# Five shared PSUM banks, one score task per chunk, and a new order of the work in a fused recurrence and feed-forward kernel

## The chip, the cores and the metric

The kernel runs on one core of a Trainium2 chip. The metric is device time in microseconds (us) of one execution; the median of three runs of the kernel before is 558.45 us (557.92 to 558.87). The core has a matrix engine (PE, with its weight loads shown apart as PEld), a vector engine (DVE), a scalar engine for activation functions (ACT), GpSimd (POOL) and a queue that issues transfers (SP). Matmuls write to PSUM, which has eight banks of 128 partitions by 512 fp32 values; DVE and ACT take results out of them.

## The reference

For each batch `b` (4) and head `h` (8) a linear recurrence runs over 768 steps with state 48 by 48, and its output tokens pass through a feed-forward net.

```python
mag = np.sqrt(a_re * a_re + a_im * a_im)
scale = np.minimum(mag, 0.999) / (mag + 1e-06)
a_re_n, a_im_n = (a_re * scale, a_im * scale)
for t in range(S):
    ar, ai = (a_re_n[:, :, t, :, None], a_im_n[:, :, t, :, None])
    new_re = ar * S_re - ai * S_im
    new_im = ar * S_im + ai * S_re
    S_re, S_im = (new_re + k_t v_t^T, new_im)
    y[:, :, t] = q_t @ S_re
...
h = x @ w_in                                       # 3072 x 384 by 384 x 2048
g = np.maximum(h, 0.0) + np.log1p(np.exp(-np.abs(h)))
return (g @ w_out).astype(np.float32)              # back to 3072 x 384
```

(The line with `k_t v_t^T` and the one with `q_t` stand for two einsums.)

## The kernel before, in words

**Tiling.** The 768 steps are cut into six groups of 128 steps. A group holds four chunks (one per batch) of 128 tokens, and after its four chunks the feed-forward net runs on the group's 512 tokens. The complex decay is turned into logarithms and angles by DVE and ACT (`pre`), which scale and rotate q and k; then a chunk is a small attention (`chunk`), and the group's 512 tokens go through `moe`.

**A chunk**, in the tiles' names: q and k are gathered by transfers into a room `qk`; k is transposed into `kt`. The scores of heads 0 to 3 and 4 to 7 (`score`, L655 in the first group, L659 later) are two tasks, each into one PSUM bank `att`. DVE multiplies a bank by a mask into `a` (`maskf`, L686). In all groups but the first, two small pieces of the bank go back into `qk`: the diagonal ones through DVE (`diag`, L674), the others by a copy that ACT or DVE does (`plain`, L696 or L679). Odd and even heads use other partitions, so each of the two is issued once for each parity. `ymm` (L722 and L726) forms the chunk's output, ACT or DVE copies its high part to `xt` (L745 or L744), DVE subtracts for the low part (L746). `kvmm` (L772 and L778) updates the state `s` (L787 or L790). Chunk matmuls after the first group have 32 output rows each (128*32 or 96*32 in the profile); the others use all of the array (128*128).

**The feed-forward net** is done in split precision. `mm1` has nine 128x512 matmuls (L817) for each of 16 slices `f` of the inner width, into a bank `h`. ACT takes abs, exp and log of it (L821 to L823), DVE reads the bank once more and completes the softplus (L832, or L826 in the first group), after which the bank is free; the result is split into `gh` and `gl` (L834 to L836). `mm2` has nine matmuls per slice (L852), accumulated over all 16 slices in three banks `o`. In the first group slices use an fp32 form (L849) instead. `filler` (L894) is a matmul whose result nobody uses.

**PSUM.** Eight banks: three `o`, two `h` and three `att` (`NATT = 3`).

**Order.** The functions only list tasks with their data dependences. `Planner.order` issues them in the sequence of a long list of numbers, `ORDER`: a number is a task, a suffix A or D moves it to ACT or DVE, `x` and `y` are fillers of 128 and 512 columns. Every engine then works strictly in that order, and waits by semaphores. When a task first uses a buffer it takes the slot that has been free longest, so the list also sets which bank a task gets. Durations given to `add` describe tasks to whoever makes the list, and change nothing in the program itself.

Of the kernel before, what the change touches and what calls it, by code (L numbers as in the profile page):

```python
# [40 lines left out]
NATT = 3  # L41
# [11 lines left out]
def slot(h):  # L53
    return h if h >= 6 else NI * (h % 2) + h // 2
# [115 lines left out]
class Prog:  # L170
# [39 lines left out]
    def masks(self):  # L210
# [15 lines left out]
        def copy():  # L226
# [6 lines left out]
            for room in FIXED["qk"]:  # L233
                G.memset(room[:QT, NI:], 0.0)
# [107 lines left out]
    def pre(self, si):  # L342
# [200 lines left out]
        return (arctan, a1(W), [t3]), (sincos, 2 * a1(W) + 0.05, [t4, t3]), turn, tail  # L543
# [4 lines left out]
    def chunk(self, si, c):  # L548
# [24 lines left out]
        if gc == 2:  # L573
            add("POOL", 3.0, lambda: nc.gpsimd.memset(qk()[:QT, NI:], 0.0), w=[(room, "z")])
# [10 lines left out]
        def heads(y):  # L585
            nc.sync.dma_start(qk()[QT * y : QT * y + 2 * D, 3 * y : 3 * y + 3].rearrange("p h n -> p (h n)"),
                              half()[D * y : D * y + D].rearrange("r (j n) -> r j n", j=2))

        def shared(y):
            nc.sync.dma_start(qk()[QT * y : QT * y + 2 * D, 6 + y],  # L590
                              half()[96 + 16 * y : 112 + 16 * y].rearrange("r (a n) -> r a n", a=2 * NI))
# [51 lines left out]
        am = []  # L643
        for j in range(2):
            psc = Buf(ps, "att", [P, 512], F32, f"sc{gc}_{j}", NATT)
            a = Buf(p, "g", [P, 4, P], F32, f"a{gc}_{j}", NG)
            am.append(a)

            def score(j=j, psc=psc):
                q = qk()  # L650
                for hh in range(4):
                    h = 4 * j + hh
                    r, k = slice(0, P if h % 2 else 2 * D), slot(h)
                    if first:
                        PE.matmul(psc()[:, hh * P : (hh + 1) * P], q[r, k, CH:], q[r, k, :CH], start=True, stop=True)  # L655
                        continue
                    for u in range(NQ):
                        f = QT * (u if h % 2 else NQ - 1 - u)
                        PE.matmul(psc()[QT * u : QT * (u + 1), hh * P + f : (hh + 1) * P],  # L659
                                  q[r, k, CH + f : CH + f + QT], q[r, k, f:CH], start=True, stop=True)  # L660

            def rows(t, z):
                return t[(P - QT, 0)[z] : (P, QT)[z]]

            def early(z, o, n, j=j):
                a, b = slot(4 * j + z), slot(4 * j + 2 + z)
                return rows(qk(), z)[:, a : b + 1 : b - a, o : o + n]

            def part(z, o, n, psc=psc):
                return rows(psc(), z).rearrange("p (x z t) -> p x z t", z=2, t=P)[:, :, z, o : o + n]  # L670
# [10 lines left out]
            def maskf(psc=psc, a=a):  # L681
                if first:
                    V.tensor_tensor(a(), psc().rearrange("p (x t) -> p x t", x=4),
                                    self.mask[:, 1][:, None].to_broadcast([P, 4, P]), ALU.mult)
                    return
                V.tensor_tensor(a()[:, :, : P - QT].rearrange("p (x z) t -> p x z t", z=2),  # L686
# [584 lines left out]
```

## Time and profile before

| | |
|---|---|
| median of three runs | 558.45 us |
| the profiled execution | 558.57 us, span 556.9 us |
| PE busy | 537.8 us (97%) |
| DVE busy | 451.8 us (81%) |
| ACT busy | 442.0 us (79%) |
| mean DMA rate | 155 GB/s |
| first feed-forward matmul | 52.76 us |
| last feed-forward matmul | 549.36 us |

Busy time of PE counts a matmul from its start to a modelled end, and neighbours overlap: how fast PE moves is read from the distance between starts. A wait in the profile is the idle time of an engine in front of an instruction, put down to what released it. A wait that a weight load (PEld) makes can be covered by matmuls that still run.

### The profile page before, as it was taken

The numbers are of one execution on the slowest core, as the hardware profiler recorded it, in microseconds if no ns is written. First come the engines' busy times: TensorE is split into PE (matmuls) and PEld (weight loads), VectorE is DVE, ScalarE is ACT, GpSimd is POOL, SyncE is SP. The second block draws the span as 40 slices with busy tenths as digits, with TensorE's granted clock in tenths as the row PEclk, the third lists the DMA queues.
The fourth block names the chain that finished last, engine by engine and source line by source line (L and its number), as shares of the span: only waits on it lengthen the run. The fifth ranks groups of instructions, "written<-read, shape, count | busy, mean of one in ns | idle before, by whom it ended". The sixth has DMA issues, their size and how long they took to land.

```text
span 556.9 us, 13372 instructions
## 1 busy us (share of the span) xinstructions
PE 537.8 (97%) x5432; PEld 419.1 (75%) x5432; DVE 451.8 (81%) x785; ACT 442.0 (79%) x776; POOL 10.5 (2%) x35
## 2 busy tenths in 40 slices
PE   4999999999999999999999999999999999999994
PEld 2689656756778887888887888788887888888883
DVE  5999999998989999998999989898898455433350
ACT  7995998788799998987987669858784665668792
POOL 7000000000000000000000000000000000000000
PEclk8899999999999999999999999999999999999998
DMA  8779905536346365176473473763626431045541
GB/s 313 278 195 312 400 26 125 204 119 189 111 159 173 131 172 189 54 189 200 105 229 89 116 189 84 192 195 112 150 75 177 128 86 58 28 126 145 157 140 61
DMA packets 49586, 86.04 MB, mean 155 GB/s; under 512 B 10224, under 2 KB 30448, under 8 KB 49520
## 3 DMA queue, kind: packets, MB, share of 16 engines
q1 hardware_dynamic: 49376, 84.89, 50.5%
q8 instruction: 43, 0.70, 0.5%
q10 hardware_dynamic: 144, 0.26, 0.1%
q14 instruction: 23, 0.19, 0.1%
HBM read 55.25 MB, written 7.86 MB: 113 GB/s over the span
## 4 chain that ended last, share of the span: by engine, by line
PE 46%; DVE 11%; ACT 3%; issue 1%; DMA 1%; SPq 0%; ACTq 0%; DVEq 0%
PE o L852 20%; PE h L817 20%; PE att L659 2%; DVE lt L832 2%; PE att L722 2%; DVE t L442 1%; DVE gl L836 1%; PE att L726 1%; DVE qk L679 1%; DVE kt L624 1%; PE att L778 1%; DVE qk L674 1%; DVE a L686 1%; ACT L945 1%; DMA qk<-x 1%
## 5 line engine op out<-in xcount | busy, mean ns | idle before, releaser
L817 PE MATMUL h<-xt,wi 128*128 128x512 f32 x864 | 216.6, 399 | 1.5 <-DVE lt L832 1.2
L817 PEld LDWEIGHTS h<-xt,wi 128*128 128x128 f32 x864 | 159.7, 188 | 42.9 <-DVE lt L832 4.5
L852 PE MATMUL o<-gh,wo 128*128 128x512 f32 x480 | 159.6, 396 | 0.0
L852 PEld LDWEIGHTS o<-gh,wo 128*128 128x128 f32 x480 | 90.1, 188 | 21.6 <-ACT o L876 0.2
L821 ACT ACTIVATE lt<-h 128x512 f32<-128x512 f32 x96 | 56.6, 592 | 62.5 <-PE h L817 54.3
L832 DVE SCALAR_TENSOR_TENSOR lt<-h,lt 128x512 f32<-128x512 f32 x80 | 54.5, 685 | 52.6 <-ACT lt L823 52.5
L852 PE MATMUL o<-gl,wo 128*128 128x512 f32 x240 | 94.4, 393 | 0.0
L823 ACT ACTIVATE lt<-lt,fixed 128x512 f32<-128x512 f32 x96 | 68.4, 718 | 1.7
L836 DVE TENSOR_TENSOR gl<-lt,gh 128x512 fp32r<-128x512 f32 x80 | 54.4, 684 | 8.9 <-ACT gh L835 4.1
L822 ACT ACTIVATE lt<-lt 128x512 f32<-128x512 f32 x96 | 59.9, 628 | 1.7
L852 PEld LDWEIGHTS o<-gl,wo 128*128 128x128 f32 x240 | 45.1, 188 | 10.2
L945 ACT ACT_TABLE_LOAD x34 | 43.6, 1283 | 0.6
L849 PE MATMUL o<-gf,raw_wo 128*128 128x512 f32 x96 | 43.2, 594 | 0.0
L442 DVE TENSOR_TENSOR_SCAN t<-hold,t 128x384 f32<-128x384 uint8 x40 | 36.1, 944 | 0.8
L659 PEld LDWEIGHTS att<-qk 128*32 128x32 f32 (+1 forms) x1280 | 25.2, 110 | 9.1 <-issue 3.7
L849 PEld LDWEIGHTS o<-gf,raw_wo 128*128 128x128 f32 x96 | 18.0, 190 | 18.5 <-issue 17.2
L659 PE MATMUL att<-qk 96*32 96x32 f32 (+7 forms) x1280 | 27.8, 234 | 1.2 <-DVE qk L679 0.5
L686 DVE TENSOR_TENSOR a<-att,mask 128x384 f32<-128x384 f32 x40 | 21.5, 543 | 3.4 <-PE att L659 1.7
L834 DVE TENSOR_SCALAR gh<-lt 128x512 fp32r<-128x512 f32 x49 | 20.3, 418 | 4.7 <-PE o L852 3.5
L540 DVE TENSOR_TENSOR x<-x,t 128x768 f32<-128x768 f32 x24 | 22.7, 950 | 0.3
L538 DVE TENSOR_TENSOR x<-x,t 128x768 f32<-128x768 f32 x24 | 22.5, 948 | 0.0
L722 PE MATMUL att<-qk,s 128*32 128x128 f32 x640 | 22.5, 274 | 0.0
(118 smaller groups left out, 720.9 us busy)
## 6 DMA issues: line engine op xcount, KB each, us to landing
x<-dense_dram SPq DMA_DIRECT2D x20, 768.0 KB, 6.6
qk<-x SPq DMA_DIRECT2D x48, 288.0 KB, 3.8
raw_wi<-w_in_dram SPq DMA_DIRECT2D x8, 768.0 KB, 10.1
raw_wo<-w_out_dram SPq DMA_DIRECT2D x8, 768.0 KB, 10.1
seen<-w_in_dram SPq DMA_DIRECT2D x16, 384.0 KB, 3.8
seen<-w_out_dram SPq DMA_DIRECT2D x16, 384.0 KB, 3.4
v<-vpad_dram SPq DMA_DIRECT2D x24, 224.0 KB, 3.9
qk<-x SPq DMA_DIRECT2D x48, 96.0 KB, 3.3
```

Of the source, the lines that this page charges most:

```text
L442: V.tensor_tensor_scan(out()[:, s], self.hold, inc()[:, s], 0.0, ALU.mult, ALU.add)
L659: PE.matmul(psc()[QT * u : QT * (u + 1), hh * P + f : (hh + 1) * P], q[r, k, CH + f : CH + f + QT], q[r, k, f:CH], start=True, stop=True)
L722: PE.matmul(o(G), s[:, w : w + 32], q[:, slot(h), :CH], start=prim and G < 4, stop=False)
L817: PE.matmul(h()[:, :n], w()[:, q, i, fs], xt()[:, x, i], start=k == 0, stop=k == 3 * NI - 1)
L821: add("ACT", a1(n) - 0.04, lambda: A.activation(tv(), h(), AF.Abs), r=[h], w=[t])
L822: add("ACT", a1(n), lambda: A.activation(tv(), tv(), AF.Exp, scale=-1.0), w=[t], tab="log")
L823: add("ACT", a1(n, 1), lambda: A.activation(tv(), tv(), AF.Ln, bias=self.one), w=[t], tab="log")
L832: add("DVE", d1(n), lambda: V.scalar_tensor_tensor(tv(), h(), 0.0, tv(), ALU.max, ALU.add), r=[h], w=[t])
L836: add("DVE", d1(n), lambda: V.tensor_tensor(gl(), tv(), gh().bitcast(F32), ALU.subtract), r=[t, gh], w=[gl])
L849: PE.matmul(acc[m]()[:, :n], v, gt[0](), start=f == 0, stop=f == NF - 1)
L852: PE.matmul(acc[m]()[:, :n], w()[:, wq, f % 2, ms], x(), start=f == 0 and q == 0, stop=f == NF - 1 and q == 2)
L945: nc.scalar.preload_act_table_set(TABLES[table])
```

## The change

1. `NATT` is 5: the `h` tiles of the feed-forward net and the attention tiles take banks from one pool of five. In the first group the running sums take a bank of it too.
2. A chunk's scores are one task into two banks, one for even and one for odd heads. `maskf`, `diag` and `plain` work on a parity each, so that `diag` and `plain` are one instruction of four heads where they were two of two heads. For that `slot` lays out `qk` by parity; `kslot` keeps the old layout for `kt`.
3. Durations told to the planner are changed in five places.
4. `ORDER` is another list.

```diff
-NATT = 3
+NATT = 5
...
 def slot(h):
+    return H // 2 * (h % 2) + h // 2
+
+
+def kslot(h):
     return h if h >= 6 else NI * (h % 2) + h // 2
...
-                lb, vl, opener = sums(0, c, "h" if first else "att", 2 if first else NATT, (part(t1, c), v1))
+                lb, vl, opener = sums(0, c, "att", NATT, (part(t1, c), v1))
...
         for j in range(2):
-            psc = Buf(ps, "att", [P, 512], F32, f"sc{gc}_{j}", NATT)
-            a = Buf(p, "g", [P, 4, P], F32, f"a{gc}_{j}", NG)
-            am.append(a)
...
+            psc.append(Buf(ps, "att", [P, 512], F32, f"sc{gc}_{j}", NATT))
+            am.append(Buf(p, "g", [P, 4, P], F32, f"a{gc}_{j}", NG))
+
+        def score():
+            q = qk()
+            for h in range(H):
+                r, k, o = slice(0, P if h % 2 else 2 * D), slot(h), h // 2 * P
...
+                for u in range(NQ):
+                    f = QT * (u if h % 2 else NQ - 1 - u)
+                    PE.matmul(psc[h % 2]()[QT * u : QT * (u + 1), o + f : o + P],
+                              q[r, k, CH + f : CH + f + QT], q[r, k, f:CH], start=True, stop=True)
...
-            def diag(early=early, part=part):
-                for z in range(2):
-                    V.tensor_tensor(early(z, 0, QT), part(z, 0, QT),
-                                    rows(self.mask, z)[:, z, :QT][:, None].to_broadcast([QT, 2, QT]), ALU.mult)
+            def diag(j=j, early=early, part=part, rows=rows):
+                V.tensor_tensor(early(0, QT), part(0, QT),
+                                rows(self.mask)[:, j, :QT][:, None].to_broadcast([QT, 4, QT]), ALU.mult)
 
             def plain(copy, early=early, part=part):
-                for z in range(2):
-                    copy(early(z, QT, P - QT), part(z, QT, P - QT))
...
+                copy(early(QT, P - QT), part(QT, P - QT))
...
-            h = Buf(ps, "h", [P, 512], F32, "h", 2)
+            h = Buf(ps, "att", [P, 512], F32, "h", NATT)
...
-149 5 8 9 10 4 2 3 24 11 12 0 1 43 27 28 62 13 46 14 65 47 30 29 31 15 16 7 929 955 32D 33 49 48 6 935 25 34 17 66
+7 149 10 11 0 12 1 13 14 3 2 4 6 5 26 29 30 32 15 45 64 48 16 31 33 907 49 17 34D 51 50 67 18 35 19 36 20 68 908 37
...
```

What the new list does is seen in the instructions of each engine. PE at the first feed-forward matmuls, before (`h_584` and so on are PSUM tiles, `wi0` to `wi2` weight blocks, `gf` a finished softplus slice, L894 the filler):

```order
L772 MATMUL att2_96<-v3_436,kt3_495 128x48
L817 MATMUL h_584<-xt_0_418,wi0_416 128x512 x9
L817 MATMUL h_595<-xt_0_418,wi0_416 128x512 x9
L894 MATMUL o0_205<-ident_58 128x128 x3
L817 MATMUL h_628<-xt_0_418,wi1_573 128x512 x9
```

and now:

```order
L770 MATMUL att1_95<-v3_178,kt3_518 128x48
L815 MATMUL att4_98<-xt_0_431,wi0_429 128x512 x9
L815 MATMUL att3_97<-xt_0_431,wi0_429 128x512 x9
L815 MATMUL att0_94<-xt_0_431,wi2_513 128x512 x9
L815 MATMUL att2_96<-xt_0_431,wi1_569 128x512 x9
L815 MATMUL att1_95<-xt_0_431,wi1_569 128x512 x9
L847 MATMUL o0_197<-gf_658,raw_wo0_228 128x512
```

Five slices now go ahead into five banks where two did, and the three fillers behind the second slice are gone.

DVE where the last tokens of the first group's `xt` are finished, before (`bits_wi5`, `bits_wo1` are weights in conversion, `a3_0` and `a3_1` the masked scores of the last chunk):

```order
L683 TENSOR_TENSOR a3_0_516<-att2_96,mask_63 128x512
L683 TENSOR_TENSOR a3_1_518<-att1_95,mask_63 128x512
L285 SCALAR_TENSOR_TENSOR bits_wi1_484<-raw_wi1_189,bits_wi1_484 128x768
L278 TENSOR_SCALAR bits_wi5_569<-raw_wi5_198 128x768
L278 TENSOR_SCALAR bits_wo1_575<-raw_wo1_446 128x768
L746 TENSOR_TENSOR xt_0_418<-y0_523,xt_0_418 128x3x128
L746 TENSOR_TENSOR xt_0_418<-y3_544,xt_0_418 128x3x128
```

and now:

```order
L685 TENSOR_TENSOR a3_1_506<-att1_95,mask_63 128x512
L685 TENSOR_TENSOR a3_0_508<-att4_98,mask_63 128x512
L282 TENSOR_SCALAR bits_wo1_563<-raw_wo1_439 128x768
L289 SCALAR_TENSOR_TENSOR bits_wi1_423<-raw_wi1_224,bits_wi1_423 128x768
L744 TENSOR_TENSOR xt_0_431<-y0_528,xt_0_431 128x3x128
L744 TENSOR_TENSOR xt_0_431<-y3_545,xt_0_431 128x3x128
L282 TENSOR_SCALAR bits_wi5_571<-raw_wi5_441 128x768
```

One weight conversion has moved from in front of the last `xt` to behind it.

DVE at a chunk of the third group, before (`a11` the masked scores, `qk0` the chunk's room):

```order
L686 TENSOR_TENSOR a11_1_2413<-att1_95,mask_63 128x4x96
L674 TENSOR_TENSOR qk0_92<-att1_95,mask_63 32x2x32 x2
L679 COPY qk0_92<-att1_95 32x2x96 x2
```

and now:

```order
L676 TENSOR_TENSOR qk1_93<-att2_96,mask_63 32x4x32
L687 TENSOR_TENSOR a11_1_2396<-att2_96,mask_63 128x4x96
L676 TENSOR_TENSOR qk1_93<-att1_95,mask_63 32x4x32
L687 TENSOR_TENSOR a11_0_2403<-att1_95,mask_63 128x4x96
```

Pairs of two-head instructions have become single four-head ones, and in this chunk the copy has left DVE for ACT.

## Rows read from the trace of the kernel before

**Rows 1.** The page: busy time and share of the span.

```profile
PE 537.8 (97%) x5432; PEld 419.1 (75%) x5432; DVE 451.8 (81%) x785; ACT 442.0 (79%) x776; POOL 10.5 (2%) x35
```

**Rows 2.** Windows by stage: stretch, its length, busy time by engine, granted clock, DMA.

```profile
53.00:148.00 95.00, 93.34 (x927) 61.19 (x926) 90.10 (x140) 82.48 (x138) 0.00 (x0) 1.00 0.53 173
148.00:226.00 78.00, 76.72 (x1021) 61.80 (x1020) 73.95 (x130) 70.46 (x123) 0.00 (x0) 1.00 0.52 160
226.00:314.00 88.00, 87.22 (x1031) 70.97 (x1032) 83.45 (x143) 72.76 (x112) 0.00 (x0) 1.00 0.53 144
314.00:400.00 86.00, 85.59 (x1002) 69.98 (x995) 78.11 (x137) 66.83 (x107) 0.00 (x0) 1.00 0.56 156
400.00:550.00 150.00, 149.76 (x1105) 120.91 (x1103) 80.06 (x157) 106.52 (x213) 0.00 (x0) 1.00 0.37 110
```

**Rows 3.** Chain that ended last, 217 to 232 us: start, duration, what.

```profile
219.51 2.10 PE o L852 x9
221.61 0.71 PE att L778 x37
```

**Rows 4.** Timeline of 47.5 to 53.3 us: start, duration, instruction.

```profile
51.07 0.56 DVE L278 TENSOR_SCALAR bits_wo<-raw_wo 128x768 int32<-128x768 int32 x1
51.16 1.77 PE L772 MATMUL att<-v,kt 128*128 128x48 f32 x16
51.54 1.08 DVE L746 TENSOR_TENSOR xt<-y,xt 128x384 fp32r<-128x384 f32 x2
52.76 0.70 PE L817 MATMUL h<-xt,wi 128*128 128x512 f32 x2
```

**Rows 5.** Timeline of PE alone, 0 to 75 us.

```profile
52.76 4.43 PE L817 MATMUL h<-xt,wi 128*128 128x512 f32 x18
57.02 0.83 PE L894 MATMUL o<-ident 128*128 128x128 f32 x6
57.92 4.45 PE L817 MATMUL h<-xt,wi 128*128 128x512 f32 x18
```

**Rows 6.** Timeline of 56 to 58.5 us: the bank's reader, the wait.

```profile
57.18 0.69 DVE L826 SCALAR_TENSOR_TENSOR gf<-h,lt 128x512 f32<-128x512 f32 x1 [0.16 <-ACT lt L823]
57.92 0.75 PEld L817 LDWEIGHTS h<-xt,wi 128*128 128x128 f32 x4 [0.26 <-DVE gf L826]
```

**Rows 7.** Timeline of PE, 254 to 264 us: into and out of 32-row matmuls.

```profile
255.37 2.26 PE L817 MATMUL h<-xt,wi 128*128 128x512 f32 x9
257.56 0.77 PE L659 MATMUL att<-qk 96*32 96x32 f32 x32
258.14 1.06 PE L722 MATMUL att<-qk,s 128*32 128x128 f32 x32
...
260.11 0.77 PE L659 MATMUL att<-qk 96*32 96x32 f32 x32 [0.24 <-DVE a L686]
260.81 0.50 PE L852 MATMUL o<-gh,wo 128*128 128x512 f32 x1
```

**Rows 8.** Waits of PE, 53 to 550 us: total, times, longest.

```profile
PE att L778 <- issue: 1.6, 1, 1.6
PE h L817 <- DVE lt L832: 1.2, 4, 0.5
PE att L659 <- DVE qk L679: 0.5, 1, 0.5
PE att L659 <- DVE a L686: 0.5, 2, 0.3
```

**Rows 9.** Waits of DVE, 53 to 314 us.

```profile
DVE lt L832 <- ACT lt L823: 2.6, 6, 0.6
DVE a L686 <- PE att L659: 1.7, 2, 1.5
DVE gl L836 <- PE o L852: 1.3, 3, 0.7
DVE qk L674 <- PE att L659: 0.6, 1, 0.6
```

**Rows 10.** Groups of DVE by form: count, busy us, mean ns.

```profile
L674 DVE TENSOR_TENSOR qk<-att,mask 32x64 f32<-32x64 f32 x80 | 17.7, 221 | 2.4 <-PE att L659 0.8 <-ACT qk L696 0.2
L679 DVE COPY qk<-att 32x192 f32<-32x192 f32 x34 | 12.0, 354 | 1.7 <-PE att L659 1.1
L790 DVE TENSOR_TENSOR s<-s,att 128x384 f32<-128x384 f32 x16 | 8.7, 543 | 0.0
```

**Rows 11.** Timeline of DVE, 311 to 316 us.

```profile
313.95 0.54 DVE L746 TENSOR_TENSOR xt<-att,xt 128x384 fp32r<-128x384 f32 x1
```

**Rows 12.** Timeline of PE, 313 to 316.5 us.

```profile
315.25 1.43 PE L817 MATMUL h<-xt,wi 128*128 128x512 f32 x5
```

**Rows 13.** Windows of the start, columns as in Rows 2.

```profile
10.00:12.00 2.00, 0.00 (x0) 0.00 (x0) 2.00 (x6) 2.00 (x7) 1.61 (x2) 0.50 1.01 415
14.00:16.00 2.00, 2.00 (x5) 0.92 (x5) 2.00 (x4) 1.97 (x6) 0.00 (x0) 0.50 1.01 409
```

More of the change, by code (lines that the diff above doesn't have):

```diff
@@ L541, in tail @@
                     r=[t4], w=r1)
[L543 removed]
+        return (arctan, a1(W), [t3]), (sincos, 2 * a1(W) + 0.1, [t4, t3]), turn, tail
     def trig(self, fn, dur, bufs):
@@ L641, in chunk @@
             add("SP", 2.0, back, r=[kd], w=[k2], nbytes=5 * NQ * NI * 2 * QT * P, parts=NQ)
-        am = []
+        am, psc = [], []
         for j in range(2):
-            psc = Buf(ps, "att", [P, 512], F32, f"sc{gc}_{j}", NATT)
-            a = Buf(p, "g", [P, 4, P], F32, f"a{gc}_{j}", NG)
-            am.append(a)
[L649 to L670, printed above, removed]
-            def diag(early=early, part=part):
-                for z in range(2):
-                    V.tensor_tensor(early(z, 0, QT), part(z, 0, QT),
-                                    rows(self.mask, z)[:, z, :QT][:, None].to_broadcast([QT, 2, QT]), ALU.mult)
@@ new lines, in chunk, with rows, early, part @@
+        add("PE", 1.8 if first else 1.17, score, r=[(room, z) for z in (0, 1, 2, 3, "z")], w=psc, mode=0 if first else 1)
+        for j in range(2):
+            def rows(t, j=j):
+                return t[(P - QT, 0)[j] : (P, QT)[j]]
+            def early(o, n, j=j, rows=rows):
+                return rows(qk())[:, slot(j) : slot(j) + 4, o : o + n]
+            def part(o, n, j=j, rows=rows):
+                return rows(psc[j]()).rearrange("p (x t) -> p x t", x=4)[:, :, o : o + n]
+            def diag(j=j, early=early, part=part, rows=rows):
+                V.tensor_tensor(early(0, QT), part(0, QT),
+                                rows(self.mask)[:, j, :QT][:, None].to_broadcast([QT, 4, QT]), ALU.mult)
@@ L685, in maskf @@
                     return
-                V.tensor_tensor(a()[:, :, : P - QT].rearrange("p (x z) t -> p x z t", z=2),
-                                psc().rearrange("p (x z t) -> p x z t", x=2, z=2)[..., QT:],
-                                self.mask[:, None, :, QT:].to_broadcast([P, 2, 2, P - QT]), ALU.mult)
-            add("PE", 0.9 if first else 0.585, score,
-                r=[(room, z) for z in ((0, 1, 2, 3, "z") if j else (0, 1, "z"))], w=[psc], mode=0 if first else 1)
-            add("DVE", d1(512 if first else 4 * (P - QT)), maskf, r=[psc, self.masked], w=[a])
@@ L693, in chunk @@
-            if not first:
-                add("DVE", 2 * d1(2 * QT), diag, r=[psc, self.masked], w=[(room, ("d", j))])
-                n = 2 * (P - QT)
-                x = add("ACT", 2 * a1(n) - 0.1, lambda plain=plain: plain(lambda o, x: A.activation(o, x, AF.Copy)),
-                        r=[psc], w=[(room, ("c", j))])
-                x.alt["DVE"] = (2 * d1(n), lambda plain=plain: plain(V.tensor_copy))
+                V.tensor_tensor(am[j]()[:, :, : P - QT], x[..., QT:],
+                                self.mask[:, j, QT:][:, None].to_broadcast([P, 4, P - QT]), ALU.mult)
@@ new lines, in chunk @@
+            add("DVE", d1(512 if first else 4 * (P - QT)), maskf, r=[psc[j], self.masked], w=[am[j]])
+            if not first:
+                add("DVE", d1(4 * QT), diag, r=[psc[j], self.masked], w=[(room, ("d", j))])
+                n = 4 * (P - QT)
+                x = add("ACT", a1(n) - 0.05, lambda plain=plain: plain(lambda o, x: A.activation(o, x, AF.Copy)),
+                        r=[psc[j]], w=[(room, ("c", j))])
+                x.alt["DVE"] = (d1(n), lambda plain=plain: plain(V.tensor_copy))
@@ L737, in chunk @@
                 add("SP", 0.45, values, w=[(sp, z)], nbytes=4 * QT * VW)
-        add("PE", 0.9 if first else 1.57, ymm, r=[room, vt] + am + ([] if first else [sp]), w=[y], mode=1)
+        add("PE", 0.9 if first else 1.59, ymm, r=[room, vt] + am + ([] if first else [sp]), w=[y], mode=1)
         off = b * CH
@@ L779, in kvmm @@
                                   stop=h == H - 1 or (h == H - 2 and u == 0))
-            add("PE", 1.33 if first else 0.6, kvmm, r=[k2 if turned else kt, vt] + ([] if first else [vo]), w=[kv], mode=0 if first else 1)
+            add("PE", 1.44 if first else 0.675, kvmm, r=[k2 if turned else kt, vt] + ([] if first else [vo]), w=[kv], mode=0 if first else 1)
             def reals(t):
```

177 lines of the change are left out of this document (91 added, 86 removed), and 3 rows, old and new, of the table ORDER.

## The prediction

> **What bounds the kernel now.** I read the page's busy times first: PE is busy 97% of the span, DVE 81%, ACT 79% [rows 1]. Such shares are averages, so next come the windows by stage [rows 2]. From 53 us, where the feed-forward net starts, to 550 us PE stands idle for 1.66, 1.28, 0.78, 0.41 and 0.24 us, 4.4 us in all, at a granted clock of 1.00 in every window. DVE is idle for 4.90, 4.05 and 4.55 us of the first three (13.5 us in 261), for 7.9 us of the next, and for 70 us of the last. So PE sets the time nearly everywhere, and up to about 314 us DVE is hardly looser than PE: what PE multiplies there, DVE has just finished. The chain of waits [rows 3] gives PE's pace, 9 matmuls in 2.10 us, 0.233 us each. The change leaves the number of attention and feed-forward matmuls alone. It can only move the start of the feed-forward net, take idle time and switches out of PE, or put new waits in.
>
> **The start.** The first feed-forward matmul starts at 52.76 us, when the last `xt` is complete at 52.62 and a `kvmm` that began at 51.16 has just let PE go [rows 4]. In the new order one weight conversion fewer stands on DVE in front of the last `xt`; 51.07 to 51.54 is its spacing, 0.47 us. But the `kvmm` still stands directly ahead of the feed-forward net, so the gain lies between 0 and 0.47, and I take 0.2 us. Two more clears of PSUM banks at the start run while PE waits for DVE and ACT anyway: PE is idle from 10 to 12 us [rows 13]. Uncovered they could not cost more than their own length there.
>
> **Five banks for two at 57 us.** Two slices of nine matmuls from 52.76 end their pace at 52.76 + 18 x 0.233 = 56.95; the third starts at 57.92, behind three fillers [rows 5]. What it really waits for is its bank: DVE reads that from 57.18 to 57.87, and the weight load names that reader [rows 6]. Five slices now run ahead, into five banks, with no filler among them. That is 0.97 us at most, I take 0.9.
>
> **Later waits for banks.** The same wait, of L817 for the DVE line that empties `h`, stands in PE's list with 1.2 us in four times [rows 8]. With five banks in turn the reader has three more slices of time, 3 x 2.1 us. I take all 1.2; the bound below is 0, since chunk tiles share the five and can hold one up as before. In the other direction `att` waits, 0.5 and 0.5 us there, may grow, for now a chunk's scores need two banks at once.
>
> **Switches between 128-row and 32-row outputs.** Before a score task, nine matmuls from 255.37 should hand over at 257.47, and the scores start at 257.56: 0.09 us. A half chunk of scores takes 0.58 us (257.56 to 258.14) when other 32-row matmuls follow, and 0.70 (260.11 to 260.81) when 128-row ones do: 0.12 us more [rows 7]. A round trip is 0.21 us. Counted in the order of PE's instructions there are 32 of them before and 26 now, since a chunk's two score tasks are one: 6 x 0.21 = 1.3 us. The scores themselves are the same matmuls in the same sequence of heads, into two banks in turn; I cost that at nothing, and if it matters the half chunk's 0.58 us is its measure.
>
> PE's own sum is thus 0.2 + 0.9 + 1.2 + 1.3 = 3.6 us less. It holds only if DVE delivers.
>
> **DVE's side.** An instruction's cost in a row of them is its mean less the overlap seen above (0.56 long, 0.47 apart: 0.09). A two-head `diag` is 0.221 - 0.09 = 0.13 us, 80 of them. The four-head form has 128 elements a row and isn't in the trace: it costs at least 0.13 and at most the 0.45 of a 384-element instruction. On the line between those two, 64 elements more are 0.06, so I take 0.20 (nearest to the two-head row). The copies go from 34 of 0.265 on DVE to 8 of 0.46, by the 384-element row [rows 10]; ACT has 32 longer ones for 46, with 12 us idle in the first window alone to cover it [rows 2].
>
> What counts is where this work lies. I counted DVE's instructions up to the last `xt` of the fourth group: 492 before, 467 now. `diag` falls from 48 to 24 (6.2 to 4.8 us), copies from 12 to 3 (3.2 to 1.4 us). Against that other work has come forward (weight splits, output and transpose evacuations that now fall to DVE, less some moved back), which priced in the same way adds 2.1 us. So only 1.1 us less lies ahead of that `xt`. It was complete at 313.95 + 0.54 = 314.49 [rows 11], and PE took it up at 315.25 [rows 12].
>
> PE now gets there with more left to do: nine `mm2` matmuls (2.1 us), one chunk's scores (1.16) and one chunk's `kvmm` (about 0.7, [rows 3]), less one switch (0.2): 3.8 us. If DVE loses as much idle time as before, PE starts this group at about 313.5, 1.8 us earlier, has 3.8 us more to do, saves perhaps 0.3 us of bank waits, and ends 1.7 us later than before. So whichever is later decides: PE's side (3.6 less) or DVE's (1.7 more, less what DVE sheds of its 13.5 us idle).
>
> How much does it shed? DVE's waits there are for the softplus chain behind PE (2.6 us), for scores (1.7 and 0.6) and for `mm2` to free a buffer (1.3): 6.2 us in which DVE was early and PE late [rows 9]. Where DVE becomes the later one such waits shorten by themselves. I take two thirds, 4.2 us, which puts DVE's side at 1.7 - 4.2 = -2.5 us. That is the later side, and so the forecast: 558.57 - 2.5 = 556.1 us for the profiled execution (span 556.9 and 1.7 around it), 0.1 less for the median, **556.0 us**. The end stays as it is: the last store follows the last matmul in both.
>
> **The rivals.**
>
> *DVE becomes the bound.* Place: the groups' first feed-forward matmuls between 148 and 315 us, and `mm2` tasks that follow their softplus more closely. Price: 1.7 us more, 560.2 us. It decides if DVE sheds less than 0.6 us of its idle time. For it: DVE's windows are 95% full, and the new order brings only 1.1 us of relief by then. Against it: 57 fewer DVE instructions up to the last group's `xt`, each a possible wait.
>
> *Nearly all idle time goes.* PE's remaining visible waits, 1.6 us for "issue" and 0.5 + 0.5 for `att` banks [rows 8], vanish as well, and DVE sheds 1.7 + 6.2 = 7.9 of 13.5 us. Time: 3.6 + 2.6 = 6.2 us less, 552.3 us. Against it: "issue" names no wait of the data, and nothing in the change touches it.
>
> *No change.* Banks weren't what PE waited for; the waits named L832 or `gf` reappear behind ACT or DVE under another name, and DVE's side happens to stand near zero: 558.4 us.
>
> *The clock falls.* After PE's idle time ahead of 12 us the granted clock is 0.50, that is 1.2 GHz, in the windows of 10 to 12 and 14 to 16 us [rows 13]; it is 1.00, 2.4 GHz, in all later windows, though banks were cycled through there too [rows 2]. A stretch of 6 us at half clock inside the feed-forward net would cost 3 us and leave 558.45 - 2.5 + 3 = 559.0 us. The Trainium skill ("TensorE: Matmul & The Clock Gate", section "A second HAM failure mode: psum-queue depth-cycling") tells of a kernel in which cycling through PSUM banks let PE idle briefly between groups and the clock swing between the two levels. By that rule a deeper cycle of banks could bring this about; the trace speaks against it, with 1.00 throughout.
>
> **How the numbers follow.** Chances: the forecast 0.50, DVE as the bound 0.25, nearly all idle time gone 0.15, no change 0.08, the clock 0.02. A measurement of this kernel can tell about 0.2%, 1.1 us, from no change, so faster means under 557.3 and slower over 559.6. The forecast's own range, with DVE shedding between 3 and 5.3 us, is 554.9 to 557.2, and wider with the bounds of the bank and start terms: 554.0 to 557.8, of which I put 0.05 into the band of no change. So faster 0.45 + 0.15 = 0.60; same 0.05 + 0.08 + 0.05 (of the slow rival) = 0.18; slower 0.20 + 0.02 = 0.22. The range that leaves 0.2 outside reaches from the best rival to the worst: 552.0 to 560.6 us.
>
> **What would show it.** In the profile of the changed kernel: a first feed-forward matmul at 52.3 to 52.8 us; five slices from there with no gap at the third; no wait of the feed-forward line for the DVE line that empties its bank; DVE idle for under 10 us between 53 and 314 us; `diag` near 0.29 us long at 40 times; the fourth group's first matmul near 310 us. It would be wrong if PE's weight loads or matmuls wait for `xt`, `gl` or masked scores by more than 2 us in all, if the start comes after 53.5 us, or if scores into two banks take over 0.62 us per half chunk.

## The result, and the profile after

The changed kernel takes 552.09 us (median of six runs, 550.50 to 553.03) against 558.32 us for the kernel before, run beside it (six runs, 557.92 to 558.87): a ratio of 0.9885, interval 0.9868 to 0.9902. That is 6.2 us less, where 2.5 were forecast. The profiled execution took 553.03 us, with a span of 551.3.

Lines have moved by a few: L815 is `mm1` (L817 before), L847 and L850 `mm2`, L661 the scores, L720 and L724 `ymm`, L776 `kvmm`, L687 `maskf`, L676 `diag`.

The page's busy times, answering to [rows 1]:

```profile
PE 533.4 (97%) x5428; PEld 419.7 (76%) x5428; DVE 441.6 (80%) x728; ACT 436.1 (79%) x755; POOL 10.3 (2%) x35
```

The same windows by stage as [rows 2], with the same columns:

```profile
53.00:148.00 95.00, 94.99 (x933) 62.39 (x932) 93.85 (x141) 78.48 (x125) 0.00 (x0) 1.00 0.54 175
148.00:226.00 78.00, 75.59 (x1018) 62.72 (x1017) 74.07 (x126) 66.60 (x112) 0.00 (x0) 0.98 0.54 158
226.00:314.00 88.00, 88.00 (x977) 72.78 (x977) 84.39 (x135) 74.40 (x113) 0.00 (x0) 1.00 0.56 155
```

PE is idle for 0.01 us of the first window and for none of the third. The second stands out: 2.41 us idle, and the only granted clock under 1.00. DVE is idle for 1.15, 3.93 and 3.61 us, 8.7 in all for 13.5 before.

The timeline of PE from 52 to 68 us, answering to [rows 4, 5], shows five slices (45 matmuls) with no gap at the third:

```profile
50.80 1.77 PE L770 MATMUL att<-v,kt 128*128 128x48 f32 x16
52.39 10.74 PE L815 MATMUL att<-xt,wi 128*128 128x512 f32 x45
62.98 2.74 PE L847 MATMUL o<-gf,raw_wo 128*128 128x512 f32 x6
```

All waits of PE's matmuls from 52 to 550 us, answering to [rows 8]; none for a bank or for data is left (a weight load of L815 still shows 0.8 us, for DVE's L788):

```profile
PE att L720 <- issue: 2.3, 1, 2.3
PE att L776 <- issue: 0.9, 1, 0.9
```

The largest waits of DVE from 53 to 314 us, answering to [rows 9], which had 6.2 us in four lines:

```profile
DVE xt L744 <- ACT xt L743: 1.2, 1, 1.2
DVE s L788 <- PE att L720: 1.1, 1, 1.1
DVE t L437 <- ACT x L436: 0.9, 2, 0.6
DVE lt L830 <- ACT lt L821: 0.9, 2, 0.5
DVE gl L834 <- PE o L850: 0.8, 1, 0.8
```

Groups of DVE by form, answering to [rows 10]: the four-head `diag` takes 285 ns.

```profile
L676 DVE TENSOR_TENSOR qk<-att,mask 32x128 f32<-32x128 f32 x40 | 11.4, 285 | 2.2 <-ACT qk L694 1.5
L680 DVE COPY qk<-att 32x384 f32<-32x384 f32 x8 | 4.4, 554 | 0.1
```

The fourth group, answering to [rows 11, 12]: first DVE, then PE. The last `xt` is complete at 304.65 us, and PE comes to it 1.8 us later, having done nine `mm2` first.

```profile
304.10 0.55 DVE L744 TENSOR_TENSOR xt<-att,xt 128x384 fp32r<-128x384 f32 x1
```

```profile
304.40 0.39 PE L850 MATMUL o<-gh,wo 128*128 128x512 f32 x1
...
306.46 1.78 PE L815 MATMUL att<-xt,wi 128*128 128x512 f32 x7
```

One thing is worse than before. In the timeline of PE, 213 to 219 us, a task stops in its middle, and windows of 2 us ahead of it, around it and behind it show the granted clock fall:

```profile
213.49 0.87 PE L720 MATMUL att<-qk,s 128*32 128x128 f32 x24
216.69 0.31 PE L720 MATMUL att<-qk,s 128*32 128x128 f32 x4 [2.33 <-issue]
```

```profile
210.00:212.00 2.00, 2.00 (x117) 1.83 (x119) 1.97 (x4) 0.49 (x2) 0.00 (x0) 1.00 0.99 369
212.00:214.00 2.00, 2.00 (x96) 2.00 (x89) 1.94 (x6) 1.56 (x3) 0.00 (x0) 1.00 0.96 365
214.00:216.00 2.00, 0.36 (x15) 0.09 (x4) 1.97 (x4) 0.99 (x2) 0.00 (x0) 1.00 0.49 134
216.00:218.00 2.00, 1.31 (x36) 1.31 (x39) 0.66 (x2) 0.00 (x0) 0.00 (x0) 0.72 0.05 11
218.00:220.00 2.00, 2.00 (x15) 1.43 (x8) 0.96 (x3) 1.32 (x3) 0.00 (x0) 0.50 0.08 12
220.00:222.00 2.00, 2.00 (x10) 1.61 (x9) 2.00 (x4) 0.35 (x1) 0.00 (x0) 0.92 0.72 129
```

Where the 6 us went is read from the starts of PE's matmuls, since their ends are modelled. The table sums the distance from each start to the next after 52.0 us, by whether both matmuls have 128-row outputs, both 32-row outputs, or one of each (a trip is one stretch of 32-row work, in and out). Runs of the next section are in it.

| kernel | trips | 128 to 128, us | 32 to 32, us | across, us | sum, us |
|---|---|---|---|---|---|
| before | 29 | 414.0 | 69.0 | 14.7 | 497.7 |
| five banks only | 29 | 412.0 | 67.3 | 14.9 | 494.2 |
| new tasks, old list | 29 | 413.4 | 72.3 | 17.1 | 502.8 |
| after | 23 | 411.5 | 69.2 | 11.1 | 491.8 |
| after, one load later | 23 | 410.0 | 66.3 | 11.0 | 487.3 |
| the last, 13 trips more | 36 | 408.6 | 66.0 | 18.2 | 492.8 |

### The profile page after: what moved, and what is told of

It reads as the page before. It is cut to its first block, busy times and chain, and to the rows that moved or that the text cites. A ratio compares the mean times of both kernels' runs of the same rounds, so it can differ in the third digit from the quotient of the medians.

```text
span 551.3 us, 13282 instructions
## 1 busy us (share of the span) xinstructions
PE 533.4 (97%) x5428; PEld 419.7 (76%) x5428; DVE 441.6 (80%) x728; ACT 436.1 (79%) x755; POOL 10.3 (2%) x35
## 4 chain that ended last, share of the span: by engine, by line
PE 79%; DVE 11%; ACT 5%; issue 2%; DMA 1%; SPq 0%; DVEq 0%; ACTq 0%
PE att L815 32%; PE o L850 29%; PE att L661 3%; PE o L847 3%; PE att L720 3%; PE att L724 2%; DVE t L446 2%; PE att L776 1%; PE att L657 1%; PE att L770 1%; PE att L609 1%; DMA x<-dense_dram 1%; ACT L943 1%; DVE a L687 1%; PE o L892 1%
## 5 line engine op out<-in xcount | busy, mean ns | idle before, releaser
L815 PE MATMUL att<-xt,wi 128*128 128x512 f32 x864 | 213.2, 398 | 0.0
L815 PEld LDWEIGHTS att<-xt,wi 128*128 128x128 f32 x864 | 161.8, 189 | 40.4 <-issue 2.2
L850 PE MATMUL o<-gh,wo 128*128 128x512 f32 x480 | 159.9, 396 | 0.0
L850 PEld LDWEIGHTS o<-gh,wo 128*128 128x128 f32 x480 | 90.1, 188 | 20.9
L850 PE MATMUL o<-gl,wo 128*128 128x512 f32 x240 | 94.3, 393 | 0.0
L819 ACT ACTIVATE lt<-att 128x512 f32<-128x512 f32 x96 | 55.5, 588 | 38.6 <-PE att L815 26.5
L830 DVE SCALAR_TENSOR_TENSOR lt<-att,lt 128x512 f32<-128x512 f32 x80 | 54.0, 686 | 39.2 <-ACT lt L821 39.1
L834 DVE TENSOR_TENSOR gl<-lt,gh 128x512 fp32r<-128x512 f32 x80 | 54.3, 687 | 21.8 <-PE o L850 14.9
L850 PEld LDWEIGHTS o<-gl,wo 128*128 128x128 f32 x240 | 45.1, 188 | 9.9
L847 PE MATMUL o<-gf,raw_wo 128*128 128x512 f32 x96 | 43.4, 596 | 0.0
L694 ACT ACTIVATE qk<-att 32x384 f32<-32x384 f32 x32 | 15.0, 479 | 22.4 <-PE att L661 16.7
L847 PEld LDWEIGHTS o<-gf,raw_wo 128*128 128x128 f32 x96 | 17.7, 190 | 18.4 <-issue 17.0
L661 PEld LDWEIGHTS att<-qk 128*32 128x32 f32 (+1 forms) x1280 | 24.2, 110 | 4.9 <-issue 2.8
L661 PE MATMUL att<-qk 96*32 96x96 f32 (+7 forms) x1280 | 26.0, 234 | 0.0
L687 DVE TENSOR_TENSOR a<-att,mask 128x384 f32<-128x384 f32 x40 | 21.5, 551 | 5.3 <-PE att L661 3.6
L833 ACT ACTIVATE gh<-lt 128x512 fp32r<-128x512 f32 x31 | 19.2, 624 | 8.0 <-PE o L850 4.1
L720 PE MATMUL att<-qk,s 128*32 128x128 f32 x640 | 22.4, 274 | 2.3 <-issue 2.3
```

What stands on the lines that cost most here:

```text
L661: PE.matmul(psc[h % 2]()[QT * u : QT * (u + 1), o + f : o + P], q[r, k, CH + f : CH + f + QT], q[r, k, f:CH], start=True, stop=True)
L720: PE.matmul(o(G), s[:, w : w + 32], q[:, slot(h), :CH], start=prim and G < 4, stop=False)
L815: PE.matmul(h()[:, :n], w()[:, q, i, fs], xt()[:, x, i], start=k == 0, stop=k == 3 * NI - 1)
L819: add("ACT", a1(n) - 0.04, lambda: A.activation(tv(), h(), AF.Abs), r=[h], w=[t])
L830: add("DVE", d1(n), lambda: V.scalar_tensor_tensor(tv(), h(), 0.0, tv(), ALU.max, ALU.add), r=[h], w=[t])
L834: add("DVE", d1(n), lambda: V.tensor_tensor(gl(), tv(), gh().bitcast(F32), ALU.subtract), r=[t, gh], w=[gl])
```

## The experiments

The theory to be tested was the forecast's: banks and fewer trips relieve PE, and DVE, with little slack, decides how much is left. The rivals: banks alone do it; DVE's shorter list of instructions does it; the new list does it, whatever the tasks. (The new list with the old score tasks was not run, so this last rival is tested from one side only.) Ratios are to the kernel before, run in turn with each.

**Five banks alone.** The list and the score tasks of before, with one pool and, as in the change, the running sums of the first group in it (two clears of banks more at the start):

```
-NATT = 3
+NATT = 5
...
-            h = Buf(ps, "h", [P, 512], F32, "h", 2)
+            h = Buf(ps, "att", [P, 512], F32, "h", NATT)
```

> The kernel before with its own list of tasks and its own score tasks, but one pool of five PSUM banks in place of two and three. Theory 'banks' (PE's loss was waiting for a feed-forward bank to be emptied; start to start, feed-forward matmuls lose 2.9 us between 145 and 430 us in the trace of before, more than the 1.2 us of idle time that the list of waits shows): 2.5 to 3.5 us less, 555 to 556 us, and no wait of L817 for the DVE line that reads h. Theory 'list' (the new sequence earns nearly all): 0 to 1.2 us less, 557.1 to 558.3 us, other waits taking the place of those for banks.

Measured: 555.23 us (554.83 to 556.55), ratio 0.9944 (0.9922 to 0.9965), 3.1 us less. Its waits of PE from 52 to 550 us:

```profile
PE att L726 <- issue: 2.2, 1, 2.2
PE att L722 <- ACT lt L823: 0.2, 1, 0.2
PE att L817 <- DVE lt L832: 0.2, 1, 0.2
```

The bank waits of [rows 8] shrink to 0.2 us. The weight loads' wait for the same reader shrinks less, from 4.5 us to 2.4. So the pool is worth half the gain, with no other list and no other task.

**`diag` and `plain` by two heads again**, in the changed kernel (40 `diag` become 80, 8 copies on DVE become 16):

```
-                V.tensor_tensor(early(0, QT), part(0, QT),
-                                rows(self.mask)[:, j, :QT][:, None].to_broadcast([QT, 4, QT]), ALU.mult)
+                for i in (0, 2):
+                    V.tensor_tensor(early(0, QT)[:, i : i + 2], part(0, QT)[:, i : i + 2],
+                                    rows(self.mask)[:, j, :QT][:, None].to_broadcast([QT, 2, QT]), ALU.mult)
```

> The changed kernel with its own list, but diag and plain as two instructions of two heads each again (40 more diag instructions and 8 more copies on DVE, 32 more on ACT, about 2.6 + 0.6 us of DVE time, 2.6 us of ACT time). Theory 'DVE relief' (DVE is nearly as tight as PE, and fewer instructions on it are what lets PE run): 1.5 to 3 us more, 553.6 to 555.1 us. Theories 'list' and 'banks' (DVE has room in the new order): within 0.8 us of the changed kernel, 551.3 to 552.9 us.

Measured: 551.82 us (551.17 to 553.77), ratio 0.9877 (0.9854 to 0.9899). No cost that a run can tell, though DVE is busy 444.5 us for 441.6; in the profile the fourth group's first feed-forward matmul comes at 307.3 us for 306.46. The wider form isn't what makes the kernel faster.

**The new tasks and banks in the old list.** Each chunk's two old score tasks are one, at the earlier place or where its banks and data are to be had (62 tasks are issued later than in the old list):

```
-(the list) ... score of heads 0 to 3, chunk c ... score of heads 4 to 7, chunk c ...
+(the list) ... score of chunk c ...
-(the list) maskf, diag, plain of heads 0 to 3, of heads 4 to 7
+(the list) maskf, diag, plain of even heads, of odd heads
```

> The changed kernel's tasks and five banks, run in the sequence of the old list (a chunk's scores at the place of its second score task; what waits for them is moved behind them, 62 tasks are issued later than the old list had them). Round trips into 32-row matmuls stay at 32. Theory 'list': 556.5 to 558.5 us, hardly better than before or no better, since scores come later for the first four heads. Theories 'banks' and 'DVE relief' (banks and single instructions earn most): 553 to 555 us.

Measured: 563.64 us (562.93 to 564.76), ratio 1.0097 (1.0074 to 1.0120): 8.4 us slower than five banks alone, and outside both theories' ranges. Its waits of PE:

```profile
PE att L720 <- DVE a L687: 2.2, 1, 2.2
PE att L815 <- DVE a L687: 1.3, 1, 1.3
PE att L776 <- DVE qk L676: 1.3, 1, 1.3
PE att L815 <- DVE qk L680: 1.3, 1, 1.3
PE att L720 <- ACT qk L694: 1.2, 1, 1.2
PE att L815 <- DVE lt L830: 1.0, 3, 0.4
```

PE now waits for masked scores and for the pieces that go back into `qk`, and the trips stay at 29. In the old list the merged task saves no trip and costs waits; the fewer trips are the new list's.

**No fillers at 57 us**, in the kernel before and in the one with five banks. The edit is one number of the list:

```
-... 196 197 x3 1121 1122 ...
+... 196 197 1121 1122 ...
```

> The kernel before without the three filler matmuls behind the second feed-forward slice, nothing else. By the reading of the prediction the third slice waits for its bank, which DVE empties at 57.87 us, and the filler only stands in that wait: within 0.3 us of before, 558.0 to 558.6 us. Rival (the filler itself delays PE): 0.6 to 0.9 us less, 557.4 to 557.7 us.

Measured in the kernel before: 559.85 us (556.19 to 562.06, twelve runs), ratio 1.0013 (0.9992 to 1.0034), no change that can be told, in a spread whose cause stays open (the executions with a mean granted clock of 0.986 to 0.989 took 559.21 to 562.06 us, those with 0.990 to 0.992 took 556.19 to 559.82). Its timeline of PE, 52 to 60 us, shows what stood under the fillers:

```profile
52.18 4.43 PE L817 MATMUL h<-xt,wi 128*128 128x512 f32 x18
57.35 2.83 PE L817 MATMUL h<-xt,wi 128*128 128x512 f32 x11 [0.74 <-DVE gf L826]
```

> The kernel before with five shared banks (as in the first run of this kind, 555.2 us) and without the three 128-column fillers behind the second feed-forward slice. Theory 'the fillers are PE time once no bank wait covers them': they go from the row, 0.97 us from the 18th to the 19th matmul in before against 0.23 in a row, of which the fillers fill what the bank wait left; the time is 0.3 to 0.9 us less, 554.3 to 554.9. Rival 'the list gives it back': the next wait takes it and the time stays within 0.3 us of 555.2. Rival 'the fillers hold the clock': it falls below 0.9 in some stretch of 53 to 80 us and the time is above 556.

Measured with five banks: 555.42 us (554.10 to 556.73), ratio 0.9944 (0.9924 to 0.9965), the same as with them. The rival that the list gives it back is right here: four slices run on without a gap, and the list of PE's waits then has 0.4 us for `gf` and 0.5 us for `lt`, where it had 0.2 us for `lt`.

**DVE's slack.** In both kernels each masking of a 128x384 score bank is done twice, 40 DVE instructions more:

```
+                for _ in range(2):
                     V.tensor_tensor(a()[:, :, : P - QT]..., psc()...[..., QT:], self.mask..., ALU.mult)
```

> The kernel before with every masking of a score bank on DVE done twice: 40 instructions more, 0.47 us apart in a row, 18.8 us, about 11.3 of them ahead of the fourth group's xt. Theory 'DVE decides up to the fourth group' (the one my forecast stood on): 13.5 us of idle there, but tied to PE's results, so that little takes it up: 6 to 11 us slower, 564.5 to 569.5. Rival 'DVE has slack': waits shorten and the time rises by less than 4 us, under 562.4.

> The changed kernel with every masking of a score bank on DVE done twice, the same 18.8 us, about 11.3 ahead of the fourth group's xt, where DVE has 8.7 us idle. Theory 'DVE is now the later side': at least as much slower as the kernel before is by the same edit, 8 to 12 us, 560 to 564. Rival 'PE still sets the time, DVE has slack': less than 5 us slower, under 557.1. If the changed kernel loses less than the one before, its list gives DVE more slack; if it loses more, less.

Measured: before 575.57 us (ratio 1.0302, 1.0281 to 1.0323), 17.0 us more than the kernel before beside it (558.54); after 567.73 us (ratio 1.0157, 1.0134 to 1.0180), 15.6 us more than the changed kernel. The added instructions take 18.8 us by the recorded estimate (40 of 0.47); the pages show DVE busy for 21.2 and 20.6 us more. So both kernels pay for most of it, far more than either theory gave. The first feed-forward matmul of the fourth group moves from 315.25 to 327.77 us in the one and from 306.46 to 315.32 in the other, for an estimated 11.3 us added ahead of it. Yet DVE's idle time between the first group's last `xt` and the fourth's, which might have taken the work up, gives little of itself: it goes from 13.5 to 13.1 us in the one, from 8.1 to 5.1 in the other. DVE has next to no slack in either kernel: work added to it is paid for in the main. Two things can lie behind that, and these runs don't part them: DVE has no free time that it could use, or the second masking stands in a chain, from the scores through DVE to `ymm`, in which PE waits. Nor do they say that DVE is the later of the two, which the part on the prediction takes up.

**The stop at 214 us.** Two theories: PE runs out of instructions, or it waits for data that the trace doesn't name. A stop inside a task speaks against data. Besides, counted from the program's start, it comes behind matmul 2252 in the changed kernel and 2251 in the one with two-head `diag`; in five kernels with the old list a stop of 1.6 to 2.2 us that begins between 109 and 113 us [rows 8] comes behind 854 or 855. (The kernel with the new tasks in the old list stops there for 0.53 us, the changed one with doubled masks behind 2252 for 0.59.) Queues of the changed kernel's page:

```profile
q1 hardware_dynamic: 49376, 84.89, 51.5%
q8 instruction: 43, 0.70, 0.5%
```

The Trainium skill ("Trainium Architecture — The Big Picture", section "The software stack") gives 64 bytes to an instruction; by that figure PE's 5428 matmuls and 5428 weight loads would be an estimated 0.695 MB, and the 0.70 MB of this queue agrees. The same section has the streams loaded before the run; the trace differs, with 43 such packets of 16 KB from 33 us to the end, one of them between 206 and 217 us, where q1 moves 1266. Around 210 us SP issues two x loads of 768 KB (timeline of SP):

```profile
208.17 0.38 SPq L406 DMA_DIRECT2D x<-dense_dram  x1
208.60 0.46 SPq L732 DMA_DIRECT2D s<-vpad_dram  x1
209.10 0.43 SPq L406 DMA_DIRECT2D x<-dense_dram  x1
213.76 0.34 SPq L413 DMA_DIRECT2D v<-vpad_dram  x1
```

> The changed kernel with two places of its list altered: of the two 768 KB x loads that SP issues at 208.17 and 209.10 us, one goes ahead of three other loads (about 202.7 us), the other behind the v load of 213.76 us. All else stands. Theory 'instructions come late': PE's 2.33 us idle at 214.36 us, put down to issue, is PE waiting for its own instructions, which a queue fetches through the same 16 DMA engines that the x loads fill; then the idle goes below 0.6 us, the granted clock stays at 1.00 in 214 to 222 us, and the time is 2.5 to 4.5 us less than the changed kernel's 552.1: 547.6 to 549.6. Rival 'a data wait that the trace does not name': the idle stays over 1.5 us at the same matmuls, and the time is within 1 us of 552.1. Rival 'the loads are needed where they are': DVE or ACT wait for x and the time is over 553.

Measured: 553.36 us (552.17 to 554.08), ratio 0.9903 (0.9886 to 0.9921). The stop behind matmul 2252 is gone, but the edit spoiled the test. The load that was put forward had to wait until 208.03 us for its room, and held up the queue behind it:

```profile
208.03 0.40 SPq L406 DMA_DIRECT2D x<-dense_dram  x1
208.48 0.53 SPq L311 DMA_DIRECT2D valo<-raw_wo  x1
209.06 0.58 SPq L417 DMA_DIRECT2D vo<-vpad_dram  x1
```

The `vo` behind it was issued at 209.06 us, for 206.76 in the changed kernel, and PE waited for it, just ahead of the place in question:

```profile
PE att L776 <- DMA vo<-vpad_dram: 3.1, 1, 3.1
PE att L776 <- issue: 0.7, 1, 0.7
```

The next two pull one lever each, the loads and the density of the instructions, and the third pulls both:

```
 one load later:   -... 1319 437 509 1308 519 438 650 ...   +... 1319 509 1308 519 438 437 650 ...
 a slice between:  -... 505 480 ... 482 518 1311 1319 ...   +... 505 1311 480 ... 482 518 1319 ...
```

(437 is the x load of 209.10 us, 438 the v load of 213.76, 505 a `kvmm`, 480 a `ymm`, 1311 a slice of nine matmuls.)

> The changed kernel with one place of its list altered: the 768 KB x load that SP issues at 209.10 us goes behind the v load of 213.76 us; the other at 208.17 stays. Theory 'instructions come late': between 208 and 214 us half as much is loaded when PE runs 192 small matmuls (form 128*32 and 96*32) in 3.5 us; the 2.33 us of PE idle put down to issue goes below 1 us, the granted clock of 214 to 222 us stays at 1.00, and the time is 2 to 4.5 us under the changed kernel's 552.1: 547.6 to 550.1. Rival 'the stream itself is too dense, whatever the loads': idle stays over 1.5 us at matmul 2252 of the program and the time is within 1 us of 552.1. Rival 'the load is late then': DVE waits for x near 224 us and the time is over 553.

Measured: 548.64 us (548.18 to 548.78), ratio 0.9825 (0.9799 to 0.9850): better than both kernels, 3.5 us under the changed one. In its timeline the same place and its clock:

```profile
213.00 0.87 PE L720 MATMUL att<-qk,s 128*32 128x128 f32 x24
214.17 0.31 PE L720 MATMUL att<-qk,s 128*32 128x128 f32 x4 [0.30 <-issue]
```

```profile
214.00:216.00 2.00, 1.83 (x42) 1.54 (x43) 2.00 (x5) 1.19 (x3) 0.00 (x0) 1.00 0.82 259
216.00:218.00 2.00, 2.00 (x10) 1.64 (x9) 2.00 (x4) 1.04 (x3) 0.00 (x0) 1.00 0.88 317
```

> The changed kernel with one place of its list altered: one of the two feed-forward slices that follow the second ymm at 218.4 us goes in front of the first ymm (near 211.9 us), so that nine long matmuls (2.1 us) stand in the middle of the small ones; one round trip of tile shape more, 0.2 us. Theory 'instructions come late': PE's queue gains 2.1 us before the next 128 small matmuls, the issue idle of 2.33 us falls below 1 us, no clock drop at 214 to 222 us, and the time is 1.5 to 4 us under 552.1: 548.1 to 550.6. Rival 'a data wait that the trace does not name, or a fixed cost at that place': the idle stays over 1.5 us and the time is 552.1 to 553.3.

Measured: 551.13 us (550.06 to 551.66), ratio 0.9865 (0.9838 to 0.9891), above the theory's range. The stop and the fall of the clock are gone with the loads where they were, so the long matmuls do it too. From the second group's first feed-forward matmul to the third's it takes 75.4 us for the changed kernel's 78.8. But the slice that came early leaves new waits behind it (scores for `lt` 0.6 us, `mm2` for `gl` 0.3 us): from the third group's to the fourth's it takes 84.7 us for 83.0, and half of the gain is given back.

> The changed kernel with both edits: the x load of 209.10 us behind the v load of 213.76 us, and one feed-forward slice in front of the first ymm near 211.9 us. Theory 'instructions come late': no issue idle over 0.5 us there, the clock at 1.00, 547.5 to 549.6 us, no better than the better of the single edits by more than 1 us. Rival 'fixed cost': 552 to 553.5.

Measured: 550.87 us (550.58 to 551.28), ratio 0.9866 (0.9840 to 0.9891): neither range; the stop is gone, and the second edit's own cost stays.

The arrival of the instructions can be seen as well. In the records of the DMA queues the packet of q8 that lies nearest the stop starts at 214.24 us in the changed kernel, and at 211.98 with one load later (the queues from 214.2 to 214.3 us in the one, from 211.9 to 212.9 in the other):

```profile
q8 instruction: 1, 0.02, 60.3%
```

```profile
q8 instruction: 1, 0.02, 5.9%
```

Wherever PE stops in these kernels, it goes on 1.2 to 1.5 us after such a packet has landed:

| kernel | behind matmul | PE stops, us | packet of q8, us | from landing to PE's start, us |
|---|---|---|---|---|
| before | 854 | 110.67 to 112.25 | 109.85 to 110.83 | 1.43 |
| five banks only | 855 | 109.87 to 112.06 | 109.69 to 110.61 | 1.44 |
| after | 2252 | 214.36 to 216.69 | 214.24 to 215.20 | 1.49 |
| after, two-head `diag` | 2251 | 215.46 to 217.48 | 215.23 to 216.19 | 1.28 |
| after, masks twice | 2252 | 222.12 to 222.71 | 220.49 to 221.47 | 1.24 |
| after, one load later | 2252 | 213.87 to 214.17 | 211.98 to 212.93 | 1.25 |

In all profiles of this case there are, after 54 us, 20 stops of PE over 0.15 us that are put down to "issue", and each ends 1.24 to 1.59 us after the end of a packet of q8, though no more than 41 such packets come in those 500 us. Late instructions are thus what ended these stops. That the x loads made the packet late rests on the one lever: with one load moved it came 2.26 us earlier, while PE came to the place 0.49 us earlier, and the stop shrank by 2.03.

**The price of a trip.** The best kernel with 13 trips more:

```
 PE's tasks, 13 times:   chunk task, chunk task, slice   ->   chunk task, slice, chunk task
```

> The changed kernel with the 768 KB x load of 209.10 us behind the v load of 213.76 us (548.6 us as measured), and with 13 more changes between 32-row and 128-row outputs on PE: at 13 places the feed-forward task that followed two chunk tasks goes between them. Theory 'a round trip costs PE 0.21 us', as I priced it from 257 to 261 us of the kernel before: 13 x 0.21 = 2.7 us more, 551.3; between 550.6 and 552.0. Rival 'the 0.12 us and 0.09 us were waits or modelled ends': less than 1 us more, under 549.6. Rival 'the chunk tasks that come 2.1 us later hold DVE up': over 553, with PE waiting for DVE lines by more than 2 us.

Measured: 553.31 us (553.08 to 553.98), ratio 0.9911 (0.9895 to 0.9928), 4.7 us more than the 548.64 of one load later: no theory's range. In the kernel with one load later PE's median step is 0.326 us into 32-row outputs and 0.136 us out of them, in place of 0.231 between 128-row and 0.009 between 32-row ones, so a trip is 0.22 us and 13 are 2.9. Waits on the trace explain part of the other 1.8: 1.5 us (0.6 for `lt`, 0.4 for issue, 0.3 for `gl`, 0.2 for `xt`), where the kernel with one load later has 0.9. The price stands by the steps; by the time alone it isn't shown.

## Why the prediction was right or wrong, step by step

*Start.* 0.2 us taken, 52.76 to 52.39 measured, but no run shows it as a gain. Kernels whose lists begin like the changed one's start between 51.86 and 53.02 us (one load later, a slice between), and the kernel before without the three fillers at 52.18. The spread is wider than the term.

*The third slice at 57 us.* 0.9 us taken. The gap is gone, and the wait under the fillers was the bank's, as said: 0.74 us without them. But filling that place alone gives nothing in the end (five banks with and without fillers: 555.2 and 555.4).

*Later bank waits: too small.* I took the 1.2 us of idle that [rows 8] names. Five banks are worth 3.1 us, only 0.3 of it at 57 us (five banks start the third slice 4.85 us after the first, before 5.16). The row that I should have set beside it is the weight loads' wait for the same reader, in the kernel before:

```profile
PEld h L817 <- DVE lt L832: 4.5, 10, 1.0
```

Ten waits of 4.5 us, where the matmuls show four of 1.2. The truth lies between, at 2.8 us. The Trainium skill ("Perfetto Trace Analysis", section "Tensor Engine Instruction (MATMUL, LD_WEIGHTS)") says that a matmul's reported end is an estimate; the trace agrees, since matmuls 0.231 us apart are shown 0.39 us long, and idle in front of the next is short by the difference.

*Trips.* 6 x 0.21 = 1.3 us, and 29 became 23 at 0.22 each. The recorded counts, 32 and 26, are of the whole program, the table's of the time after 52.0 us. Right in number and, by the steps, in price; wrong in reason: I wrote "since a chunk's two score tasks are one", and with one task in the old list there are still 29.

*DVE's side: the step that failed.* I took it for "the later side, and so the forecast", at 2.5 us less. Measured on DVE from the first group's last `xt` to the fourth group's: 261.9 us before, 252.6 after. Of those 9.3 us, 5.4 are idle time (13.5 to 8.1, where I let it shed 4.2), 2.2 are busy time (I had 1.1), and the rest is closer overlap of neighbours. PE reached the fourth group's feed-forward 8.8 us earlier, not 6.0, and then had 2.9 us more to do, where I had 3.8 less 0.3. And DVE wasn't the later side. The prediction's own rows speak against it: the `xt` of [rows 11] was complete 0.76 us before PE took it up [rows 12], and PE was not idle then but in a score task, so to reckon PE's start of the group (313.5 us, 1.8 earlier) from DVE's end was a misreading. The row that shows it, from the same timeline:

```profile
314.55 0.77 PE L659 MATMUL att<-qk 96*32 96x32 f32 x32
```

In the changed kernel no matmul after 52 us waits for data. (That its `xt` is complete 1.8 us before PE comes to it says little by itself: nine `mm2` stand between by the list, and with doubled masks the distance is still 1.6 us.) When one load later took 3.5 us out of PE, DVE followed, with the same `xt` 4.1 us earlier (300.6 us) and 4.9 us idle in place of 8.1. DVE's idle was mostly PE's lateness, so it shrinks as far as PE hurries; a fixed share of it was a guess. What stands of the step is that there is no slack to lose: an added DVE microsecond costs most of one, as the doubled masks show.

*PE's own sum* was too small as well, 3.6 us for 6.2 measured, so that without DVE's step the forecast would still have been 2.6 short. Five banks (3.1 us measured, 0.9 + 1.2 taken) and six trips (1.3) make 4.4 of it. The other 1.8 come with the new list; no run takes them apart.

*Issue and the clock: not foreseen.* I wrote that "nothing in the change touches" the issue wait. It does: the new list puts a score, a `kvmm` and two `ymm` in a row at the time of two x loads. The stop of 2.33 us and the half clock behind it cost 3.5 us in the median, against the version with one load later. The clock need not fall in each execution: the changed kernel's six lie in the order of their mean granted clock, from 550.50 us at 0.998 to 553.03 at 0.991, and only the last was profiled. My rival on the clock named the wrong cause: the rule of the Trainium skill ("TensorE: Matmul & The Clock Gate", section "A second HAM failure mode: psum-queue depth-cycling") would have the short idle times of PE that come with cycling through banks bring the clock down, and the trace disagrees: with five banks cycled all the time the clock is 1.00 in the first and the third window above, and in all three of them in the version with one load later.

*The rival "nearly all idle goes", 552.3 us,* has the right size and half the right course: bank waits and DVE's waits went, issue did not. That its 552.3 us lies 0.2 from the measured time is in part luck. The sum of PE's steps says it (after less before, from the table): 2.5 us between 128-row matmuls, although six trips fewer put 6 x 0.231 = 1.4 us of such steps in; 3.6 across, of which 6 x 0.46 = 2.8 go with the trips; nothing between 32-row ones, because the stop is in there (66.3 in place of 69.2 with one load later).

*Its own tests.* Held: first matmul at 52.3 to 52.8 us, no gap in five slices, no bank wait of PE's feed-forward line, DVE idle under 10 us, `diag` near 0.29 us. Missed: the fourth group's first matmul, 306.46 for 310.

## What to carry to other kernels

Where one engine is 97% busy and another 95% in the stage that counts, as here, don't ask which is later by the idle time of each: idle of the second was mostly lateness of the first, so price what the first loses, from the distances between its starts rather than from its visible idle (its weight loads' waits gave an upper mark: 4.5 us, where 2.8 were to be had). A merged task and a new order are two changes; run each alone before giving either the credit. A stop named "issue" inside a task is worth a look at when the instruction queue's packets land, at what is being loaded there and at how many short instructions run in a row: moving one load gave more than half as much as the whole change.

## What the runs showed of the hardware

PE can stop for want of instructions. In this case's profiles the queue named "instruction" moved 43 packets of 16 KB while the kernel ran, and each of PE's 20 stops named "issue" ended 1.24 to 1.59 us after one of them had landed. The long stops, of 1.6 to 2.3 us, came at the same matmul of the program in kernels that differ elsewhere. In six of the kernels PE had just run 81 to 122 matmuls in 2 us while the core's 16 DMA engines were 0.96 to 1.06 busy. With one of two x loads moved away 0.30 us of the stop in the changed kernel was left, and with nine long matmuls in between none. That the loads held the instruction packet up is the reading that fits both levers; no row shows the packet waiting.

The clock behind such a stop isn't fixed by its length alone. After 2.19 us idle in the kernel with five banks the granted clock stayed at 1.00, that is 2.4 GHz; after 2.02 us in the one with two-head `diag` it fell to 0.50, that is 1.2 GHz, as it did after 2.33 us in the changed kernel, where matmuls then stood 0.427 us apart in place of 0.23. Behind the stop with five banks, and behind the one with two-head `diag`:

```profile
114.00:116.00 2.00, 2.00 (x9) 1.29 (x8) 2.00 (x4) 1.99 (x3) 0.00 (x0) 1.00 0.08 31
```

```profile
220.00:222.00 2.00, 2.00 (x6) 1.52 (x6) 2.00 (x4) 0.00 (x0) 0.00 (x0) 0.50 0.45 82
```
